# Three slot lists instead of two, experts begun at unit 36, and ScalarE's queue for the rows of early slots

## The chip, the cores and the metric

The kernel runs on one core of one Trainium2 chip. The metric is the device time of one execution, in microseconds (us), lower is better. The engines are TensorE (PE in the profile, its weight loads PEld), VectorE (DVE), ScalarE (ACT), GpSimd (POOL) and SyncE (SP). SP and ACT issue ordinary DMAs, each from a queue of its own; POOL issues the indirect ones (gathers and scatters of rows).

## The reference

Banded attention, then a top-1 mixture of experts on its output. Eight batches, eight heads of 64, 576 positions; heads 0 to 3 see the last 32 positions, heads 4 to 7 every fourth of the last 128. All numbers are float32.

```
scores = np.where(masks, q @ k^T / 8, -1e9)          # per head, masked to the band
x = softmax(scores) @ v  -> [4608, 512]              # 8 batches x 576 tokens
logits = x @ w_gate + modality_bias[modality_id]     # 8 experts
e_idx = argmax(logits); gate_w = softmax(logits)[e_idx]
for e in range(8):
    m = e_idx == e
    out[m] = gate_w[m] * (relu(x[m] @ w1[e]) @ w2[e])   # w1 512x1024, w2 1024x512
```

With the given inputs only experts 1, 6 and 7 receive tokens (1621, 2290 and 697 of them).

## The kernel before

**Attention** is cut into 72 units, nine to a batch, in the order of the list `order`; a unit is 128 query rows of four heads. The loop `for t in range(NU + LAG + 1)` is a software pipeline written out by hand: in its turn t it emits the scores of unit t, the exponentials (L361, tile `pe`) of unit t-1, the transposed probabilities (`pT`, L369) of t-2, the products with v (`po`, L375) of t-3, the store of the rows to DRAM (`x_dram`, from ACT's queue) of t-4 and the gate logits (L419) of t-5. PE, DVE, ACT and SP run what is emitted in exactly that order (`manual_schedule`); POOL mostly too. Loads of q, k and v (tiles `st` and `vw`) for the next batches are issued by SP at fixed turns of a batch, `vw` in many small pieces (L138) with a shift inside SBUF behind them (L144).

**Routing.** Five turns after a batch's last unit, `background(b)` starts; the loop advances it by a step or two in each turn. `gating` finds the expert and rank of each token and scatters token numbers and weights into a DRAM table with a region per expert (POOL, L505). `slot_info` turns the counts of tokens into a list of slots: a slot is 256 tokens of one expert. There are two lists here. The early one is made behind batch 2 (`EARLY_B`), holds six full slots (`NEARLY`) and uses the tokens of batches 0 to 2; the other comes behind batch 7 and holds twelve slots and one half slot. A runtime loop after them takes what may be left.

**A slot** needs: its row of the list read into registers (`TENSOR_LOAD`), the token numbers (`idt`, from the table), four gathers of 128 half rows by POOL (`xr`), a write of these to DRAM (`x_slot`), four loads back in a layout for 32 x 32 transposes (`xg`), two transposes on DVE (`xt`), and a split into two fp32r parts (`xh`, `xl`). In the kernel before, `idt`, `x_slot` and `xg` are all issued by SP. `x_slot`, `xg` and `xr` have one buffer each. The expert's weights come in six pieces (`fetch_weights`: w2 pair 0, w1 half 0, pairs 1 and 2, half 1, pair 3) into single buffers `w1q` and `w2q`; a slot with the same expert as the slot before skips the copies.

**The experts' work** is the generator `slots`: a slot is eight chunks of 128 hidden columns, each twelve matmuls to `pt` (L806), the relu to `hh` (ACT, L812) and `hl` (DVE), and two chunks later six matmuls to `py` (L787). A chunk is four steps. From turn `T_MOE` = 49 on, `step()` weaves these into the attention, 4.4 steps a turn (`MOE_RATE`), so 1.1 chunks a unit. At the start three banks of PSUM for the attention (`ps_o`) become one, and two go to `py`. `ahead(n, f, end)` is called twice in each chunk and issues what the next slots need.

Of the kernel before, what the change touches and what calls it, by code (L numbers as in the profile page):

```python
# [23 lines left out]
NT = B * S  # L24
# [14 lines left out]
NEARLY = 6  # L39
EARLY_B = 2  # L40
NSTAT = 12
HALFF = 4
T_MOE = 49
# [21 lines left out]
def kernel(  # L65
# [379 lines left out]
    def gating(b, lT):  # L445
# [40 lines left out]
        state['counts'] = [run[:, :, 0]] + [oh[:, :, c] for c in range(NGB)]  # L486
# [13 lines left out]
        for c in range(NGB):  # L500
            if c > 0 and b < B - 1:
                yield
                if b != EARLY_B:
                    yield
# [4 lines left out]
            for before in scatters:  # L509
                tc.declare_no_dep(ins, before, reason="every token has a row of its own")  # L510
            scatters.append(ins)
# [3 lines left out]
    def slot_info(counts, early):  # L515

        ps = psum['o'].tile([P, 512], F32, name="po")
# [3 lines left out]
        ns = gwk.tile([1, 1, NE], F32, name="ns")  # L523
        if early:
            nc.vector.tensor_copy(out=cn, in_=ps[0:1, 0:NE])
            nc.vector.tensor_single_scalar(cn, cn, 8, op=ALU.arith_shift_right)
            nc.vector.tensor_copy(out=ns[:, 0, :], in_=cn)
            yield
        else:
# [6 lines left out]
            full = gwk.tile([1, NE], F32, name="full")  # L536
# [16 lines left out]
            nc.vector.tensor_tensor(out=ns[:, 0, :], in0=full, in1=done[:, 0:NE], op=ALU.subtract)  # L553
            yield
        n = NEARLY if early else NSLOT
        cs = gwk.tile([1, 1, NE], F32, name="cs")
        nc.vector.tensor_tensor_scan(out=cs[:, 0, :], data0=one8, data1=ns[:, 0, :], initial=0.0, op0=ALU.mult, op1=ALU.add)
        if early:

            d = done[:, 0:NE]  # L560
            nc.vector.tensor_tensor(out=d, in0=ns[:, 0, :], in1=cs[:, 0, :], op=ALU.subtract)
            nc.vector.tensor_scalar(out=d, in0=d, scalar1=float(NEARLY), scalar2=0.0, op0=ALU.add, op1=ALU.max)
            nc.vector.tensor_tensor(out=d, in0=d, in1=ns[:, 0, :], op=ALU.min)
        yield
# [5 lines left out]
        if not early:  # L570

            nc.vector.tensor_tensor(out=ns[:, 0, :], in0=full, in1=done[:, 1:NE + 1], op=ALU.subtract)
# [5 lines left out]
        if not early:  # L578
            nc.vector.tensor_scalar(out=bs, in0=bs, scalar1=done[:, 0:1], scalar2=None, op0=ALU.add)
        yield  # L580
        state['info_e' if early else 'info'] = slot_list(es, bs, n, "info_e" if early else "info")
# [3 lines left out]
    def rest_info():  # L585
# [5 lines left out]
        nc.vector.memset(state['info'][:, 2, NSTAT:NSTAT + 1], 1)  # L591
# [18 lines left out]
    pool.memset(done, 0.0)  # L610
    last_e = cpool.tile([1, 1], F32, name="last_e")
# [13 lines left out]
    def fetch_ids(si, after=(), nu=2):  # L625

        row = nc.sync.value_load(si[0:1, 1:2], min_val=0, max_val=(NE + 1) * NT - SLOT)
        idt = gat.tile([P, 2, 3], I32, name="idt", bufs=NEARLY)
        load = nc.sync.dma_start(out=idt[:, 0:nu], in_=table[ds(row, P * nu), :].rearrange("(p u) t -> p u t", u=nu))
        wait_all(load.ins, after)  # L630
        return idt, nu

    def gather(n, ids):
# [4 lines left out]
        nrows = (EARLY_B + 1) * S if n < NEARLY else NT + 1  # L638
# [6 lines left out]
        nc.sync.dma_start(out=x_slot[0:P * nu, :].rearrange("(u p) c -> p u c", p=P), in_=xr[:, 0:nu])  # L645
# [4 lines left out]
        for r in range(KC):  # L650
            nc.sync.dma_start(out=xg[BLK * r:BLK * (r + 1), 0:nu * KC],
                              in_=x_slot[0:P * nu, P * r:P * (r + 1)].rearrange("(g i) c -> i g c", i=BLK))
# [30 lines left out]
    early = {}  # L683
    NS = NEARLY + NSTAT + 1
    taken = set()

    def background(b):

        if b < B - 1:
            yield  # L690
        yield from gating(b, state['lT', b])
        if b == EARLY_B:
            yield
            yield from slot_info(state['counts'], True)
            for i in range(NEARLY):
                early['si', i] = slot_regs(state['info_e'], i)
            yield
            yield
            for i in range(3):
                early['ids', i] = fetch_ids(early['si', i])  # L700
                yield
            yield
            early['loads'] = fetch_weights(early['si', 0], True)
            yield from together(islice(early['loads'], 2), gather(0, early['ids', 0]))
            yield
            yield from prepare_x(0, early['ids', 0])
        elif b == B - 1:
            yield
            yield from slot_info(state['counts'], False)
            yield from rest_info()  # L710
            state['routed'] = True
# [57 lines left out]
    def slots(ns, ids_of, ahead, base=0):  # L769
# [25 lines left out]
        for n in range(ns):  # L795
            ids = ids_of[n]
            cols = P * ids[1]
            for f in range(FC):
                g = n * FC + f
                if f == 0:  # L800
                    xh, xl = state.pop(('x', base + n))
# [17 lines left out]
                if g + 2 < ns * FC:  # L819
                    split_w1(g + 2)  # L820
# [5 lines left out]
    ids_of, si_of, fetching = {}, {}, []  # L826

    def fetch_slot(n):

        if n < NEARLY:  # L830
            si_of[n] = early['si', n]
            ids_of[n] = early['ids', n] if n < 3 else fetch_ids(si_of[n])
        elif n < NS:
            half = n == NS - 1
            si_of[n] = slot_regs(state['info_h'], 0) if half else slot_regs(state['info'], n - NEARLY)
# [175 lines left out]
```

## Time and profile before

| | us |
|---|---|
| runs shown | 783.83, 777.83, 779.45 (median 779.45) |
| the profiled execution, its own time | 780.03 |
| its span in the trace | 778.3 |
| PE busy / PEld / DVE / ACT / POOL | 675.1 / 584.1 / 504.8 / 407.2 / 258.9 |
| mean granted TensorE clock | 0.919 |

The 1.7 us between the span and the time lie around the program. The profile names groups by line, engine, operation and tiles as `out<-in`; a wait is given as "engine line waited for", with the total, how often, and the longest. A window row gives the busy time of each engine in a stretch, then the granted clock, the share of the DMA engines' time, and GB/s. Units can be found in it by the exponential of each (`pe<-sm`, ACT), chunks by their relu (`hh`, ACT).

### The profile page before, as it was taken

What the parts mean: (1) busy time and instruction counts of PE and PEld (TensorE: products, weight loads), DVE (VectorE), ACT (ScalarE), POOL (GpSimd) and SP (SyncE); (2) the same over time, 40 slices, a digit from 0 to 9 for tenths busy, and PEclk for the clock granted to TensorE, in tenths of its full rate; (3) what the DMA queues carried; (4) which work ended last, traced back from release to release, by engine and by line L of the source; (5) the groups of instructions that cost most, each with busy time, mean ns of one, the idle gap of its engine ahead of it and who ended that gap; (6) DMA issues with size and microseconds to landing.
All of it is one profiled execution on the core that took longest, in us unless ns stands there. A gap on an engine that the chain in (4) does not pass through costs nothing. (4 is left out here: it accounts for less than half of the span.)

```text
span 778.3 us, 17878 instructions
## 1 busy us (share of the span) xinstructions
PE 675.1 (87%) x6286; PEld 584.1 (75%) x6286; DVE 504.8 (65%) x1216; ACT 407.2 (52%) x900; POOL 258.9 (33%) x348
## 2 busy tenths in 40 slices
PE   5898888883447999988989898999999999999995
PEld 3686767663336877776778787999999999999984
DVE  2587766682245677766857764777666677766763
ACT  3374655551324556653555364566566656656553
POOL 7323534433331433434444523233133323312100
PEclk7598988997659799999999999999999999999998
DMA  9776675759567557982322599332582333266270
GB/s 170 170 183 144 144 164 127 168 133 203 132 165 171 177 122 183 216 201 60 78 76 42 130 277 260 120 109 89 164 227 78 109 97 109 95 177 189 82 186 21
DMA packets 151009, 111.79 MB, mean 144 GB/s; under 512 B 87600, under 2 KB 124978, under 8 KB 150916
## 3 DMA queue, kind: packets, MB, share of 16 engines
q1 hardware_dynamic: 132884, 81.97, 44.6%
q0 software_dynamic: 8048, 19.20, 8.4%
q10 hardware_dynamic: 9984, 9.44, 3.7%
q8 instruction: 50, 0.82, 0.5%
q14 instruction: 43, 0.35, 0.2%
HBM read 127.52 MB, written 29.39 MB: 202 GB/s over the span
## 5 line engine op out<-in xcount | busy, mean ns | idle before, releaser
L806 PE MATMUL pt<-xh,w1h 128*128 128x256 f32 (+1 forms) x608 | 176.9, 291 | 3.5 <-ACT xh L745 3.2
L806 PE MATMUL pt<-xh,w1l 128*128 128x256 f32 (+1 forms) x608 | 172.4, 284 | 5.2 <-DVE w1l L756 4.5
L806 PE MATMUL pt<-xl,w1h 128*128 128x256 f32 (+1 forms) x608 | 172.3, 283 | 1.5 <-DVE xl L746 1.5
L812 ACT ACTIVATE hh<-pt 128x256 fp32r<-128x256 f32 (+1 forms) x152 | 57.6, 379 | 151.5 <-PE pt L806 151.1
L756 DVE TENSOR_TENSOR w2l<-w2q,w2h 128x512 fp32r<-128x512 f32 x152 | 106.1, 698 | 45.0 <-ACT w2h L755 38.0
L806 PEld LDWEIGHTS pt<-xh,w1h 128*128 128x128 f32 x608 | 115.9, 191 | 12.6 <-ACT xh L745 4.1
L284 POOL DMA_INDIRECT xr<-x_dram,idt x74 | 81.4, 1100 | 128.8 <-DMA x_slot<-xr 70.4
L787 PE MATMUL py<-w2h,hh 128*128 128x512 f32 x296 | 124.0, 419 | 0.0
L806 PEld LDWEIGHTS pt<-xl,w1h 128*128 128x128 f32 x608 | 116.2, 191 | 6.8 <-DVE xl L746 1.9
L806 PEld LDWEIGHTS pt<-xh,w1l 128*128 128x128 f32 x608 | 116.6, 192 | 6.1 <-DVE w1l L756 5.9
L787 PE MATMUL py<-w2h,hl 128*128 128x512 f32 x296 | 119.4, 403 | 0.0
L787 PE MATMUL py<-w2l,hh 128*128 128x512 f32 x296 | 117.2, 396 | 0.0
L756 DVE TENSOR_TENSOR w1l<-w1q,w1h 128x512 fp32r<-128x512 f32 x152 | 106.2, 699 | 14.2 <-ACT w1h L755 14.2
L284 POOL TENSOR_TENSOR sm<-sm,nmx 128x384 f32<-128x384 f32 x72 | 61.1, 849 | 137.6 <-DVE den L382 71.0
L813 DVE SCALAR_TENSOR_TENSOR hl<-pt,hh 128x256 fp32r<-128x256 f32 (+1 forms) x152 | 62.7, 413 | 65.8 <-ACT hh L812 65.7
L755 ACT CAST w1h<-w1q 128x512 fp32r<-128x512 f32 x152 | 94.2, 621 | 15.6 <-DMA w1q<-in_moe_w_dram 15.6
L284 POOL DMA_INDIRECT out_dram<-ys,idt x37 | 40.6, 1099 | 179.4 <-ACT ys L790 100.8
L369 ACT COPY pT<-pt 96x512 f32<-96x512 f32 x72 | 41.8, 581 | 102.5 <-PE pt L366 102.4
L755 ACT CAST w2h<-w2q 128x512 fp32r<-128x512 f32 x152 | 93.3, 614 | 0.3
L787 PEld LDWEIGHTS py<-w2l,hh 128*128 128x128 f32 x296 | 56.6, 191 | 13.7
L375 PE MATMUL po<-vw,pT 96*64 96x65 f32 x1152 | 56.1, 244 | 11.3 <-DMA vw<-vw 8.2
L375 PEld LDWEIGHTS po<-vw,pT 96*64 96x64 f32 x1152 | 45.1, 151 | 24.2 <-issue 12.1
(163 smaller groups left out, 1084.9 us busy)
## 6 DMA issues: line engine op xcount, KB each, us to landing
w2q<-in_moe_w_dram SPq DMA_DIRECT2D x76, 512.0 KB
w1q<-in_moe_w_dram SPq DMA_DIRECT2D x152, 256.0 KB
x_slot<-xr SPq DMA_DIRECT2D x18, 512.0 KB
xg<-x_slot SPq DMA_DIRECT2D x72, 128.0 KB
x_dram<-x_sb ACTq DMA_DIRECT2D x32, 256.0 KB
st<-in_k_dram SPq DMA_DIRECT2D x32, 144.0 KB
st<-in_q_dram SPq DMA_DIRECT2D x32, 144.0 KB
st<-in_k_dram SPq DMA_DIRECT2D x16, 288.0 KB
```

Of the source, the lines that this page charges most:

```text
L284: ins = tc.keep_in_program_order(getattr(nc.gpsimd, name)(*args, **kw))
L369: nc.scalar.copy(out=self.pT, in_=src)
L375: nc.tensor.matmul(out=pov[u * TQ:(u + 1) * TQ, h, :], lhsT=self.pT[:, h, u * TQ:(u + 1) * TQ], rhs=self.vts[kd][:, h, i, :], start=True, ...
L755: nc.scalar.copy(out=hi, in_=raw)
L756: nc.vector.tensor_tensor(out=lo, in0=raw, in1=hi.bitcast(F32), op=ALU.subtract)
L787: nc.tensor.matmul(out=py[u], lhsT=ht[:, us], rhs=wt, start=(f + n == 0), stop=(f + n == FC + 1))
L806: nc.tensor.matmul(out=ph, lhsT=wt[:, c, :], rhs=xt[:, c, 0:cols], start=(c + i == 0), stop=(c + i == KC + 1))
L812: nc.scalar.activation(out=hh, in_=ph, func=AF.Relu)
L813: nc.vector.scalar_tensor_tensor(out=hl, in0=ph, scalar=0.0, in1=hh.bitcast(F32), op0=ALU.max, op1=ALU.subtract)
```

## The change

- **Lists.** `EARLY = ((1, 3), (3, 5))`: a list of three slots behind batch 1 (tokens of batches 0 and 1), a list of five behind batch 3 (batches 0 to 3), and one of ten and a half slot behind batch 7. `slot_info(counts, r)` keeps in `done` how many full slots of each expert earlier lists took. The slots remain 19.
- **Start.** `T_MOE` is gone. The experts begin in the turn after `background(1)` has emitted the split of slot 0's rows (`state['go']`), which is turn 36; the kernel before began in turn 49.
- **Queues.** The token numbers of slots 0 and 1, and `x_slot` and `xg` of the eight early slots, are issued from ACT's queue instead of SP's. One more `yield` stands between the last gather of a slot and its `x_slot`.
- **Control.** `ahead` looks at what is there instead of at fixed slot numbers, and `hold` emits no expert step before its rows and weights have been emitted.

```
+EARLY = ((1, 3), (3, 5))
+NEARLY = sum(n for _, n in EARLY)
+NSTAT = 18 - NEARLY
-T_MOE = 49
...
-    def fetch_ids(si, after=(), nu=2):
+    def fetch_ids(si, after=(), nu=2, queue=nc.sync):
-        row = nc.sync.value_load(si[0:1, 1:2], min_val=0, max_val=(NE + 1) * NT - SLOT)
-        load = nc.sync.dma_start(out=idt[:, 0:nu], in_=table[...])
+        row = queue.value_load(si[0:1, 1:2], min_val=0, max_val=(NE + 1) * NT - SLOT)
+        load = queue.dma_start(out=idt[:, 0:nu], in_=table[...])
...
     def gather(n, ids):
-        nrows = (EARLY_B + 1) * S if n < NEARLY else NT + 1
+        nrows = round_rows(n)
+        queue = nc.scalar if n < NEARLY else nc.sync
...
-        nc.sync.dma_start(out=x_slot[0:P * nu, :]..., in_=xr[:, 0:nu])
+        yield
+        queue.dma_start(out=x_slot[0:P * nu, :]..., in_=xr[:, 0:nu])
         yield
...
-            nc.sync.dma_start(out=xg[BLK * r:BLK * (r + 1), 0:nu * KC], ...)
+            queue.dma_start(out=xg[BLK * r:BLK * (r + 1), 0:nu * KC], ...)
...
     def background(b):
+            yield from together(steps, slot_info(state['counts', b], round_of[b]))
+            if round_of[b] > 0:
+                return
+            yield
+            for n in range(2):
+                fetch_slot(n, nc.scalar)
+                yield
+            load_more(0, 1)
+            yield
+            rows = gather(0, ids_of[0])
+            for i, _ in enumerate(rows):
+                yield
+                if i in (1, 3):
+                    load_more(0, 1)
+            yield
+            yield from prepare_x(0, ids_of[0])
+            state['go'] = True
...
     for t in range(NU + LAG + 1):
-        if t == T_MOE:
-            run(tasks_early)
+        if 'go' in state and not moe:
...
-        if t < T_MOE or t >= NU:
-            advance()
+        advance([*round_of, B - 1] if moe and t < NU else range(-1, B))
```

**Slot 0's rows.** On SP before, this stands between the first weights of slot 0 and its rows (`st` and `vw` are loads of later batches; the loads of `xg` follow directly behind):

```order
L123 DMA st<-in_k_dram 48x12x64 x4
L123 DMA st<-in_q_dram 48x12x64 x4
L138 DMA vw_106<-in_v_dram 64x4x64 x2
L138 DMA vw_106<-in_v_dram 16x4x64
L138 DMA vw_106<-in_v_dram 48x4x64
L138 DMA vw_106<-in_v_dram 64x4x64
L138 DMA vw_106<-in_v_dram 32x4x64 x2
L138 DMA vw_106<-in_v_dram 64x4x64
L138 DMA vw_106<-in_v_dram 48x4x64
L138 DMA vw_106<-in_v_dram 16x4x64
L138 DMA vw_106<-in_v_dram 64x4x64 x2
L645 DMA x_slot<-xr 128x2x512
```

In the changed kernel the same two steps stand on ACT, about half a unit apart; the exponentials (L361) are those of units 32 and 33:

```order
L361 ACTIVATE pe<-sm 128x384
L653 DMA x_slot<-xr 128x2x512
L472 ACTIVATE ex<-ex 96x48
L369 COPY pT<-pt 96x512
L401 CAST uxh<-pt 128x256
L320 COPY kT_101<-pt 128x2x144
L318 ACTIVATE qT_100<-po 128x2x144
L659 DMA xg<-x_slot 32x8x128 x4
L361 ACTIVATE pe<-sm 128x384
```

The loads of later batches no longer stand ahead of the rows; the attention's own work now stands behind them on ACT.

**Slot 1's rows**, on ACT of the changed kernel, in the turn 38 (for slots 2 and 3 one instruction stands between the two DMAs; for slots 4 to 7 four to eight do):

```order
L361 ACTIVATE pe<-sm 128x384
L805 CAST w2h<-w2q_240 128x512
L805 CAST w1h<-w1q_238 128x512
L653 DMA x_slot<-xr 128x2x512
L659 DMA xg<-x_slot 32x8x128 x4
L863 ACTIVATE hh<-pt 128x256
L369 COPY pT<-pt 96x512
L401 CAST uxh<-pt 128x256
```

The loads of `xg`, which read what `x_slot` wrote, directly follow it, ahead of a relu and of a unit's transposed probabilities.

**The first expert matmuls**, on PE of the changed kernel against before, right behind the logits (L419) of the unit 31:

```order
 L419 MATMUL po<-uxl,wgs 16x64
-L366 MATMUL pt<-ident,pe 96x128 x4
-L397 MATMUL pt<-ident,x_sb 128x128 x2
-L312 MATMUL pt<-ident,st 128x96 x3
-L312 MATMUL po<-ident,st 128x96 x3
+L857 MATMUL pt<-xh,w1h 128x256
+L857 MATMUL pt<-xl,w1h 128x256
+L857 MATMUL pt<-xh,w1l 128x256
+L857 MATMUL pt<-xh,w1h 128x256
+L857 MATMUL pt<-xl,w1h 128x256
+L857 MATMUL pt<-xh,w1l 128x256
```

From here on the experts' matmuls (L857, L806 before) stand between the attention's; before, only attention follows here for thirteen more turns.

More of the change, by code (lines that the diff above doesn't have):

```diff
@@ L510, in gating @@
                 tc.declare_no_dep(ins, before, reason="every token has a row of its own")
+            for load in state['loads_of_ids']:
+                tc.declare_no_dep(ins, load, reason="the rows of full slots are written before")
             scatters.append(ins)
@@ L838, in ahead @@
[L838 to L852 removed]
+    todo = {'calls': 0, 'ids': 2, 'rows': 1}
```

190 lines of the change are left out of this document (100 added, 90 removed).

## The prediction

> **What bounds the kernel now.** I read the windows first, cut where the work changes; the cuts are starts of a unit's exponential (units 9, 36, 42, 48, 53, 71).
>
> ```profile
> 52.20:154.20 102.00, 84.69 (x1331) 72.56 (x1325) 71.89 (x229) 54.82 (x140) 42.86 (x67) 0.88 0.68 151
> 154.20:172.60 18.40, 16.17 (x287) 13.75 (x284) 16.95 (x67) 11.07 (x31) 7.32 (x10) 1.00 0.58 139
> 172.60:232.30 59.70, 24.12 (x309) 20.25 (x307) 18.20 (x54) 14.28 (x34) 19.18 (x25) 0.66 0.70 162
> 232.30:272.30 40.00, 35.35 (x358) 29.61 (x360) 25.44 (x65) 21.53 (x50) 12.06 (x14) 0.87 0.69 175
> 272.30:391.70 119.40, 109.45 (x1211) 90.41 (x1207) 87.32 (x220) 65.72 (x150) 44.63 (x60) 0.99 0.61 141
> 391.70:480.00 88.30, 76.65 (x508) 66.56 (x507) 58.55 (x157) 42.60 (x90) 37.79 (x41) 0.95 0.57 154
> 502.50:750.50 248.00, 248.00 (x1585) 224.11 (x1584) 174.80 (x306) 149.37 (x308) 62.09 (x56) 1.00 0.45 130
> ```
>
> Columns are length, then busy time of PE, PEld, DVE, ACT, POOL, then clock, DMA share and GB/s. PE fills the last window wholly and nine tenths of the woven ones (232.3 to 391.7). The hole is the third: 59.7 us with 24.1 us of PE work at clock 0.66, just ahead of the first expert matmul. Counts of exponentials (`pe`) and relus (`hh`) in the same windows give the rates:
>
> ```profile
> L361 ACT ACTIVATE pe<-sm x27: 514/526/532, 52.2 to 150.9; 128x384 f32<-128x384 f32 x27
> L361 ACT ACTIVATE pe<-sm x6: 514/521/532, 172.6 to 229.4; 128x384 f32<-128x384 f32 x6
> L361 ACT ACTIVATE pe<-sm x5: 514/520/526, 232.3 to 268.1; 128x384 f32<-128x384 f32 x5
> L361 ACT ACTIVATE pe<-sm x18: 514/522/535, 272.3 to 384.5; 128x384 f32<-128x384 f32 x18
> L812 ACT ACTIVATE hh<-pt x26: 363/384/392, 236.5 to 388.6; 128x256 fp32r<-128x256 f32 x26
> L812 ACT ACTIVATE hh<-pt x88: 377/385/388, 502.5 to 747.8; 128x256 fp32r<-128x256 f32 x88
> ```
>
> Attention alone takes 102.0/27 = 3.78 us a unit, the six units in the hole 9.95 each, a woven unit first 40.0/5 = 8.0 and then 119.4/18 = 6.63, and a chunk of experts alone 248/88 = 2.82. A woven unit carries 1.1 chunks, 3.1 us: weaving hides nearly nothing, since 6.63 - 3.1 = 3.5 is what attention alone costs. So thirteen more woven turns gain nothing by themselves; what can be won is the hole. The timeline says what is in it:
>
> ```profile
> 190.99 0.23 DVE L437 TENSOR_REDUCE dstf<-t 96x6 f32<-96x48 f32 x1 [9.42 <-POOL t L284]
> 192.03 0.92 PE L350 MATMUL pss<-kT,qT 64*64 64x96 f32 x16 [7.89 <-DVE sm L353]
> 187.56 1.07 POOL L284 DMA_INDIRECT xr<-x_dram,idt  x1 [15.55 <-DMA idt<-table]
> 192.56 1.01 POOL L284 DMA_INDIRECT xr<-x_dram,idt  x1 [0.16 <-DVE nmx L356]
> 224.17 0.71 DVE L739 STREAM_TRANSPOSE xt<-xg 128x512 f32<-128x512 f32 x1 [21.45 <-DMA xg<-x_slot]
> 225.25 0.29 PE L419 MATMUL po<-uxl,wgs 128*16 128x128 f32 x1 [21.16 <-DVE uxl L402]
> ```
>
> Two chains. POOL stood 15.55 us before slot 0's first gather for the token numbers; what routing asked of POOL waited behind it, DVE behind POOL, PE behind DVE: 7.89 us. Then DVE stood 21.45 us before slot 0's transpose for `xg`, and PE 21.16 us. Together 29.1 us of PE. Why the rows were late is on SP's timeline:
>
> ```profile
> 178.53 6.35 SPq L629 DMA_DIRECT2D idt<-table  x3
> 201.44 3.83 SPq L123 DMA_DIRECT2D st<-in_k_dram  x4
> 205.36 3.38 SPq L123 DMA_DIRECT2D st<-in_q_dram  x4
> 208.84 7.38 SPq L138 DMA_DIRECT2D vw<-in_v_dram  x12
> 216.39 0.46 SPq L645 DMA_DIRECT2D x_slot<-xr  x1
> 219.30 1.79 SPq L651 DMA_DIRECT2D xg<-x_slot  x4
> ```
>
> ```profile
> DMA to landing us min/median/max: 2.8/4.1/7.1
> ```
>
> The last gather was issued at 193.6 and a gather lands 4.1 us later (the row of `idt`'s readers), at 197.7; `x_slot` left SP at 216.39, 18.7 us later, behind loads of later batches.
>
> **Part by part.** The sum runs over the profiled execution: span 778.3 us, own time 780.03, 0.6 above the median of 779.45.
>
> *Up to unit 36* little changes but one more list: seven tiny matmuls and some twenty DVE operations on one partition, nearest row 0.23 us (`dstf`), so 4.6 us over five units on a DVE busy 71.89 of 102. Cost nothing, with 4.6 if that slack is not there. Unit 36 stands at **154.2**.
>
> *Slot 0's rows now go over ACT.* SP's 18.7 us and the wait for the numbers behind SP's loads go; what is late next are the transfers themselves, and now ACT waits for them, with a unit's `pT` and `uxh` behind it and PE behind these.
>
> ```profile
> DMA to landing us min/median/max: 2.9/6.1/6.9
> 231.84 0.37 ACTq L410 DMA_DIRECT2D x_dram<-x_sb  x1
> ```
>
> The first of these rows is the table's scatters, 6.1 us to land. ACT meets its first `idt` about a unit after the last scatter: 6.1 - 3.8 = 2.3 us. `x_slot` to `xg` was 219.30 - 216.39 = 2.9 us; half a unit (1.9) lies between: 1.0. Four issues of `xg` hold ACT as SP, 1.8 us (a store's issue on ACT, 0.37 us, says the same). The transpose came 224.17 - 219.30 = 4.9 us after the first issue of `xg`; with 1.9 to 3.8 us between in the new order, DVE still waits 2.0. Sum **7.1 us**; bounds 0 (these stretches are DMA-bound and have slack) and 29.1 (both old waits come back). I take 7.1, since its rows are transfers of the same size.
>
> Here one rule speaks against the change. The Trainium skill, page "DMA: Bandwidth & Descriptors", section "Issuing engines are not separate DMA queues", says that DMAs started by SyncE, ScalarE and GpSimd run on the same 16 DMA engines and interleave, and that starting them from several engines only saves the sequencer's time, which is usually small. The trace shows that time as 18.7 us here, not small; by the rule's "usually" it would have stayed and this term were 21.2 instead of 7.1, rival two.
>
> *Woven units.* From unit 36 to 71 there are 35 instead of 23. I price them as before: 40.0 for the first five, then 30 x 6.63 = 199.0: **239.0**. The loss of PSUM banks for attention is in that rate. Bounds: 35 x 6.63 = 232 and 35 x 8.0 = 280.
>
> *Rows of slots 1 to 7 over ACT.* In the order of before SP waits there and nobody cares. ACT now issues 0.4 + 1.8 = 2.2 us a slot, and for slots 1 to 3 the loads of `xg` stand at most one instruction behind `x_slot`, so ACT waits the 2.9 us too: 5.1 a slot. Behind it are a relu, a `pT` and the weight splits. PE has little in hand (three `pt` banks, shared with attention), so I count all of it, 3 x 5.1 = **15.3 us**, and nothing for slots 4 to 7, where a chunk stands between. Bounds 0 (ACT is busy 65.72 of 119.4) and 7 x 5.1 = 36; I stay at the middle, as no row shows an ACT wait of this kind. SP gains these issues, worth nothing while PE bounds.
>
> *Two more weight loads.* Slots now run 1,6,6 / 1,1,6,6,7 / 1... instead of 1,1,6,6,6,7 / 1..., so nine loads instead of seven; those of slots 1, 3 and 5 fall in the woven stretch, where one fell before.
>
> ```profile
> w2q<-in_moe_w_dram SPq DMA_DIRECT2D x76, 512.0 KB
> w1q<-in_moe_w_dram SPq DMA_DIRECT2D x152, 256.0 KB
> 440.00:460.00 20.00, 18.59 (x120) 16.41 (x119) 12.02 (x22) 10.23 (x21) 6.96 (x7) 1.00 0.95 251
> ```
>
> A load is 4 x 512 + 8 x 256 KB = 4.2 MB, 16.7 us at the 251 GB/s of a window that is nearly all weights. Two are 33 us of DMA; the woven windows leave three to four tenths of 239 us free. That hides them but for the crowd at turns 36 to 42, where slot 0's second half and slot 1's whole load meet a batch's `st` and `vw`: **3 us**, bounds 0 and 33.
>
> *The rest.* At unit 71 ACT's order has 41 relus behind it against 26, so 15 chunks fewer remain: 386.6 us of before (778.3 - 391.7) less 15 x 2.82 = 42.3: **344.3**. The end of routing keeps its place: two slots of early rows ahead of it, as before; its 88.3 us window is carried over.
>
> Sum: 154.2 + 7.1 + 239.0 + 15.3 + 3 + 344.3 = 762.9, with 1.7 around it **764.6 us**, 1.9% under the median.
>
> **Rivals.**
>
> 1. *ACT's waits are hidden.* For it: ACT idles 45% of the woven time, and its stores, which also wait, delay nobody today. Against: PE follows ACT closely there. Terms 7.1, 15.3 and 3 become 5, 0 and 0: 742.5, time 744.
> 2. *The wait only changes its place.* The transfers of slot 0's rows share the DMA engines with the loads (share 0.70 in the hole), land as late as before, and ACT or DVE stands for them: 21.2 for 7.1, span 777.0, time 779. This is the rule's case. Against it: SP's 18.7 us were spent before the transfer had been issued.
> 3. *Slower: ACT waits for SP's loads.*
>
> ```profile
> SPq L123 <- DMA x_dram<-x_sb: 32.2, 11, 11.6
> SPq L669 <- DVE w2l L756: 190.0, 58, 12.0
> ```
>
> By these rows loads on SP (L123) waited 32.2 us for stores that ACT had issued, though they share no data: DMAs of the two queues do wait for each other. SP also stands 190 us in all for DVE to free `w2q`. If ACT's `x_slot` or `xg` has to wait for a weight load or `vw` piece that SP has not yet issued, ACT, and with it PE, stands for SP. Without the 15.3 the sum is 747.6; it decides from 40 us on, 5.0 us for each of eight gathers (slower by over 1% then). At 8 us each: 747.6 + 64 + 1.7 = 813. Against it: the stores that ACT issues now show no such wait.
>
> That the change does not do what it says is unlikely: counts of the inputs fill both short lists exactly (3 and 5 full slots), and the order has experts from turn 36.
>
> **How the numbers follow.** A measurement of this kernel tells a change from none at about 1%, 7.8 us: under 771.7 is faster, above 787.2 slower. Forecast 0.48, nearly all of it under 771.7; rival one 0.20; rival two 0.19, inside 1%; rival three 0.11; the rest 0.02. Faster 0.65, same 0.22, slower 0.13. All low ends give 732, all high ends above 840; the range holds the forecast, rival one from 743 on and rival two, up to 786, and leaves out rival three and the corners.
>
> **What would show it.** Right: no PE wait above 8 us before the first expert matmul, which starts near 160; unit 71 near 419; PE waits on ACT of 2 to 5 us at slots 1 to 3 behind an ACT DMA; the last 340 us as before. Wrong: a DVE wait for `xg` of over 10 us (rival two), an ACT DMA held while SP's weight loads run (rival three), woven units well off 6.6, or the end of routing finding no slot ready.

## The result: 3.6% slower, and where the time went

The changed kernel takes **807.28 us** (median of four runs, 803.85 to 813.67); the kernel before took 779.57 beside it. The ratio is **1.0355, 95% interval 1.0293 to 1.0416**. The forecast was 764.6, so the sign was wrong. Ratios and intervals leave out single executions that lie more than 1.5% above the fastest of their kernel, among them one of e4 that took 1237.58 us, whose trace is not used. The profiled execution of the changed kernel is the longest of its four (813.67, span 811.9, 0.8% above the median). Its windows are cut at starts of unit exponentials (9, 28, 36, 38, 53, 71); the last one is a stretch of experts alone:

```profile
56.20:127.70 71.50, 59.22 (x957) 50.67 (x951) 52.57 (x183) 38.40 (x98) 29.75 (x46) 0.90 0.73 142
127.70:182.30 54.60, 34.51 (x421) 28.84 (x417) 28.02 (x81) 20.54 (x50) 20.75 (x29) 0.72 0.91 191
182.30:216.60 34.30, 12.11 (x122) 10.03 (x122) 7.69 (x20) 6.83 (x17) 5.90 (x6) 0.69 0.77 180
216.60:334.70 118.10, 103.78 (x1072) 86.90 (x1065) 77.92 (x207) 60.01 (x138) 37.52 (x47) 0.89 0.64 145
334.70:470.30 135.60, 118.92 (x1208) 98.74 (x1208) 86.56 (x224) 65.60 (x151) 46.88 (x60) 0.90 0.64 144
557.80:783.70 225.90, 225.68 (x1441) 204.33 (x1440) 158.77 (x278) 135.64 (x279) 59.68 (x54) 1.00 0.53 144
```

The same view of before, for units 28 to 36:

```profile
122.10:154.20 32.10, 25.30 (x397) 21.45 (x392) 21.71 (x70) 16.28 (x43) 14.57 (x23) 0.89 0.72 159
```

The third row after is the old hole in a new place: 34.3 us with 12.1 us of PE work at clock 0.69. The second row shows that it begins earlier: eight units take 54.6 us instead of 32.1, with nearly the same number of matmuls (421 against 397) and the clock at 0.72 instead of 0.89. Against the forecast's sum, term by term:

| stretch | forecast | measured | difference |
|---|---|---|---|
| to unit 28 | 122.1 | 127.7 | +5.6 |
| units 28 to 36 | 32.1 + 7.1 | 54.6 | +15.4 |
| units 36 to 38, first experts | 2 x 8.0 | 34.3 | +18.3 |
| units 38 to 71 | 33 of the 35 woven units (223.0), 15.3 and 3 | 253.7 | +12.4 |
| unit 71 to the end | 344.3 | 341.6 | -2.7 |
| span | 762.9 | 811.9 | +49.0 |

What stands in the first of these holes, on the timeline of the changed kernel (SP's DMA issues, then ACT, then PE):

```profile
172.88 2.46 SPq L123 DMA_DIRECT2D st<-in_k_dram  x4
175.45 5.41 SPq L123 DMA_DIRECT2D st<-in_q_dram  x4
180.96 11.60 SPq L138 DMA_DIRECT2D vw<-in_v_dram  x12
...
193.40 1.87 SPq L674 DMA_DIRECT2D w1q<-in_moe_w_dram  x4
...
203.23 0.62 ACT L805 CAST w1h<-w1q 128x512 fp32r<-128x512 f32 x1 [15.55 <-DMA w1q<-in_moe_w_dram]
203.41 0.37 ACTq L653 DMA_DIRECT2D x_slot<-xr  x1
210.88 1.88 ACTq L659 DMA_DIRECT2D xg<-x_slot  x4
212.81 0.38 ACT L863 ACTIVATE hh<-pt 128x256 fp32r<-128x256 f32 x1 [8.96 <-issue]
...
213.72 0.74 PE L312 MATMUL pt<-ident,st 96*128 96x96 f32 x3 [22.19 <-ACT pT L369]
```

ACT stood 15.55 us for the second half of slot 0's `w1`, which SP issued at 193.40, behind a batch's `st` and `vw` (172.88 to 192.56). Then ACT issued slot 1's `x_slot`, and all that follows in its order stood until `xg` could go at 210.88, 7.5 us later; by the built program this first `xg` waits for `x_slot` to land and for nothing else. PE stood for both: 22.19 us. It is the same pattern as before, a list's data behind a batch's loads, with ACT's own DMA added. The DMA engines had room until SP issued the weights, and were full from then on:

```profile
187.00:193.40 6.40, 4.53 (x44) 3.56 (x42) 1.60 (x3) 0.68 (x2) 1.14 (x1) 1.00 0.27 60
193.40:203.20 9.80, 0.00 (x0) 0.00 (x0) 0.00 (x0) 0.00 (x0) 0.00 (x0) 0.61 1.01 235
```

Through the woven units ACT stands again and again (waits of ACT from unit 38 to 71, total, times, longest; the relu is named since it is next in ACT's order):

```profile
ACT hh L863 <- DMA xg<-x_slot: 14.5, 2, 8.3
ACT hh L863 <- DMA w2q<-in_moe_w_dram: 6.6, 1, 6.6
ACT hh L863 <- DMA vw<-in_v_dram: 4.6, 1, 4.6
```

The longest of them on the timeline:

```profile
314.67 6.93 ACTq L659 DMA_DIRECT2D xg<-x_slot  x4
321.65 0.38 ACT L863 ACTIVATE hh<-pt 128x256 fp32r<-128x256 f32 x1 [8.33 <-DMA xg<-x_slot]
```

Four issues that take 1.9 us where nothing holds them took 6.9. The built program says what the later ones wait for. This is ACT's order around that place, slot 3's rows:

```
387 L653 DMA x_slot<-xr 128x2x512 [waits DMASW7_49,DMAHW5_49,DMASW6_49,DMAHW7_49,DMASW1_49,DMASW0_49]
388 L318 ACTIVATE qT_100<-pt 128x2x144 [waits PE_49]
389 L659 DMA xg<-x_slot 32x8x128 [waits DMAHW7_49,DMAHW3_49]
390 L659 DMA xg<-x_slot 32x8x128
391 L659 DMA xg<-x_slot 32x8x128 [waits DMAHW2_49]
392 L659 DMA xg<-x_slot 32x8x128 [waits DMAHW3_49]
```

A semaphore is a counter that an instruction can wait for. In this program SP's and ACT's DMAs signal their completion on eight shared ones (DMAHW0 to 7), and a DMA that is to signal on one waits until the DMA that used it last has landed, also when the other engine has yet to issue that one. Here the first `xg` waits for `x_slot` (DMAHW7) and an `st` of SP (DMAHW3), the third for a `w1q` piece, the fourth for the first `xg` itself. All but the wait for `x_slot` have nothing to do with the data.

### The profile page after: what moved, and what is told of

Its sections match the earlier page's. It is cut to its first block, busy times and chain, and to the rows that moved or that the text cites. A ratio compares the mean times of both kernels' runs of the same rounds, so it can differ in the third digit from the quotient of the medians.

```text
span 811.9 us, 17892 instructions
## 1 busy us (share of the span) xinstructions
PE 690.8 (85%) x6293; PEld 595.8 (73%) x6293; DVE 508.6 (63%) x1243; ACT 406.5 (50%) x900; POOL 260.3 (32%) x348
## 5 line engine op out<-in xcount | busy, mean ns | idle before, releaser
L857 PE MATMUL pt<-xh,w1h 128*128 128x256 f32 (+1 forms) x608 | 183.6, 302 | 16.8 <-DVE hl L864 5.9
L857 PE MATMUL pt<-xh,w1l 128*128 128x256 f32 (+1 forms) x608 | 176.6, 290 | 5.7 <-DVE left L597 5.1
L857 PE MATMUL pt<-xl,w1h 128*128 128x256 f32 (+1 forms) x608 | 176.2, 290 | 1.8 <-DVE xl L796 1.8
L857 PEld LDWEIGHTS pt<-xh,w1h 128*128 128x128 f32 x608 | 120.2, 198 | 26.5 <-DVE hl L864 6.1
L806 DVE TENSOR_TENSOR w2l<-w2q,w2h 128x512 fp32r<-128x512 f32 x152 | 104.5, 687 | 42.7 <-ACT w2h L805 36.5
L837 PE MATMUL py<-w2h,hh 128*128 128x512 f32 x296 | 126.5, 427 | 0.0
L857 PEld LDWEIGHTS pt<-xl,w1h 128*128 128x128 f32 x608 | 120.7, 198 | 6.5 <-DVE xl L796 2.3
L857 PEld LDWEIGHTS pt<-xh,w1l 128*128 128x128 f32 x608 | 120.5, 198 | 6.5 <-DVE left L597 5.3
L806 DVE TENSOR_TENSOR w1l<-w1q,w1h 128x512 fp32r<-128x512 f32 x152 | 106.7, 702 | 21.8 <-ACT w1h L805 21.8
L312 PE MATMUL pt<-ident,st 96*128 96x96 f32 x273 | 44.7, 281 | 37.1 <-ACT pT L369 27.7
L312 PEld LDWEIGHTS pt<-ident,st 96*128 96x128 f32 x273 | 34.4, 162 | 44.5 <-ACT pT L369 28.8
```

What stands on the lines that cost most here:

```text
L312: nc.tensor.transpose(out=pt[:, 2 * PQ * i:2 * PQ * (i + 1)], in_=src[:, s].rearrange("p a d -> p (a d)"), identity=ident[:2 * PQ, :2 * PQ])
L806: nc.vector.tensor_tensor(out=lo, in0=raw, in1=hi.bitcast(F32), op=ALU.subtract)
L837: nc.tensor.matmul(out=py[u], lhsT=ht[:, us], rhs=wt, start=(f + n == 0), stop=(f + n == FC + 1))
L857: nc.tensor.matmul(out=ph, lhsT=wt[:, c, :], rhs=xt[:, c, 0:cols], start=(c + i == 0), stop=(c + i == KC + 1))
```

## The experiments

All ratios are against the kernel before, run beside it on the same chip. The quoted expectations name the kernels in full (h2_after_slot0 is h2, built from the changed kernel; h1_before_slot0 is h1, built from the kernel before). Two theories come up again and again: "queue" says that the loss is ACT standing at its own DMAs, "crowd" that loads which meet in one place delay each other whatever queue they come from.

### All rows on SP, and the kernel before with rows on ACT

**Edit e1** (on the changed kernel):

```
-        queue = nc.scalar if n < NEARLY else nc.sync
+        queue = nc.sync
-                fetch_slot(n, nc.scalar)
+                fetch_slot(n, nc.sync)
```

> The changed kernel, with every DMA of the early slots issued by SP again; lists, start at turn 36 and weight loads stay. Theory 'queue' (ACT stands for x_slot and for SP's loads; the gaps ahead of ACT's idt and xg issues sum to some 36 us, and xg's issues to 14): most of that goes, 765 to 775 us, no ACT wait ahead of a DMA, and the PE wait of 22 us at 191 shrinks by the 7.5 us between x_slot and xg. Theory 'crowd' (turn 36 follows directly on a batch's st and vw loads, so the weights of slots 0 and 1 and these loads stand in each other's way whatever queue the rows take): 795 to 815, with slot 0's rows now late behind SP, as before the change, and the wait for w1q still there.

Measured 788.05, ratio 1.0071 (1.004 to 1.0102), between the ranges of both theories. The queue accounts for most of the loss. What remains around the start is the old chain, DVE's wait for `xg` (120 to 230 us) with PE 16.2 us behind it:

```profile
DVE xt L789 <- DMA xg<-x_slot: 23.3, 2, 17.6
```

**Edit e2** (on the kernel before: `x_slot` and `xg` of its six early slots and the first two `idt` on ACT):

```
+        queue = nc.scalar if n < NEARLY else nc.sync
-        nc.sync.dma_start(out=x_slot[...
+        queue.dma_start(out=x_slot[...
-            nc.sync.dma_start(out=xg[...
+            queue.dma_start(out=xg[...
```

> The kernel before (two lists, start at turn 49), with x_slot and xg of its six early slots and the first two idt issued by ACT. Theory 'queue': the waits on ACT cost more than the hole gives back, 785 to 800. Theory 'crowd': the hole of 29 us shrinks to under 10 and the rest stays, 755 to 770; then the queue was the good part of the change.

Measured 793.39, ratio 1.0107 (1.0047 to 1.0168). The hole did shrink: units 42 to 48 ran from 177.8 to 213.2, 35.4 us instead of 59.7. But units 48 to 71 took 189.7 instead of 159.4. The three largest of ACT's waits on DMAs from 170 us on:

```profile
ACT w2h L756 <- DMA w2q<-in_moe_w_dram: 14.4, 1, 14.4
ACT kT L320 <- DMA xg<-x_slot: 8.8, 2, 6.8
ACT hh L813 <- DMA xg<-x_slot: 6.5, 1, 6.5
```

The queue that shortened slot 0's wait lengthened the rest; the next two kernels take the two apart.

### Only slot 0 on ACT

**Edits h1 and h2** (h1 on e2, h2 on the changed kernel):

```
-        queue = nc.scalar if n < NEARLY else nc.sync
+        queue = nc.scalar if n < 1 else nc.sync
```

> The kernel before with only slot 0's rows (x_slot, xg) and the first two idt on ACT's queue; slots 1 to 5 stay on SP. 'Queue' (an ACT DMA of the rows holds ACT, and PE with it, wherever SP's loads are under way; only slot 0 is worth it): the hole keeps the 24 us it lost when all six slots went over ACT (units 42 to 48 in about 35 us instead of 59.7), units 48 to 71 come back from 189.7 to about 160, time near 757. 'Crowd' (the DMA engines are full, so what arrives early at one place is late at the next): the 20 us gap behind the start, where ACT waited for the first weights behind a batch's vw pieces, stays, units 48 to 71 take 175 to 190, time 772 to 785.

> The changed kernel with only slot 0's rows and the ids on ACT's queue; slots 1 to 7 on SP. 'Queue': units 36 to 38 as in the changed kernel (a gap near 20 us for the weights), then 7.1 us a unit as with everything on SP instead of 7.7: 33 x 0.6 = 19 us less, time near 788. 'Crowd': the woven units stay near 7.7, since it is the two more weight loads that fill them, time near 803. If ACT's hold of slot 0 alone were the loss of units 28 to 36, unit 36 still stands at 182.

h1 measured 772.32, ratio **0.9865** (0.979 to 0.994): faster than both kernels, though short of the 757 that "queue" expected. In its windows (units 42 to 48, then 48 to 71) the hole keeps its 25 us, and the woven part takes 175.1 instead of 159.4:

```profile
181.40:215.80 34.40, 23.32 (x304) 20.04 (x304) 17.89 (x53) 14.24 (x34) 15.12 (x21) 0.66 0.98 201
215.80:390.90 175.10, 147.73 (x1563) 122.11 (x1564) 113.58 (x284) 87.51 (x199) 56.48 (x73) 0.90 0.60 146
```

Of these 15.7 us, 15.2 are one PE gap at 233.7, where ACT waits 11.4 us for the second piece of slot 0's `w2q`, which SP issued behind a batch's loads, and then 6.2 for a `w1q`: "crowd" was right on that point.

h2 measured 783.59, ratio **1.0027** (0.9981 to 1.0073). Taking slots 1 to 7 off ACT's queue gives back 3.3% of 779.6, some 26 us of the 28 lost. Its windows (units 28 to 36, 36 to 38, 38 to 71):

```profile
124.40:178.20 53.80, 35.22 (x418) 29.74 (x416) 27.63 (x80) 20.43 (x49) 20.81 (x28) 0.71 0.98 198
178.20:203.40 25.20, 12.17 (x124) 10.10 (x123) 7.64 (x21) 6.77 (x17) 1.97 (x2) 0.78 0.74 174
203.40:437.80 234.40, 210.21 (x2270) 174.98 (x2262) 165.15 (x429) 125.89 (x287) 89.84 (x110) 0.94 0.70 163
```

The 33 woven units went from 253.7 to 234.4, 7.69 to 7.10 each. Of these 19.3 us only 6.8 are less standing of PE; in the other 12.5 PE was busy for longer on the same work (222.7 against 210.2, at clock 0.89 and 0.90 against 0.94). The profiled execution of h2 lies 0.6% below its median, that of the changed kernel 0.8% above, so the two profiles differ by more than the medians do. The start is no shorter in its first part: eight units still take 53.8.

### Which DMA holds ACT

**Edits h8, h9 and h10**, all on the changed kernel: h8 moves `x_slot` of slots 1 to 7 to SP and leaves `xg` on ACT, h10 the other way round, h9 puts two more turns between them.

```
h8   -        queue.dma_start(out=x_slot[...
     +        (queue if n < 1 else nc.sync).dma_start(out=x_slot[...
h9   +        for _ in range(2 if 0 < n < NEARLY else 0):
     +            yield
              while 0 < n < NS and n - 1 not in taken:
h10  -            queue.dma_start(out=xg[...
     +            (queue if n < 1 else nc.sync).dma_start(out=xg[...
```

> The changed kernel with x_slot of slots 1 to 7 on SP; xg of these slots, four DMAs each, stays on ACT. Slots 1 to 7 on ACT cost 24 us (after against h2_after_slot0). 'It is the wait for x_slot to land, in front of xg, and the four issues': nothing or little is gained, 800 to 807. 'It is the x_slot DMA that ACT holds for (its gathers have not landed)': most of the 24 us is gained, 783 to 789.

> The changed kernel with the xg DMAs of slots 1 to 7 issued two turns later, 8 to 16 ACT instructions behind x_slot instead of 1 to 9, still on ACT. 'Landing' (ACT waits for x_slot, 2.9 us alone and 5 to 8 us with loads running, as it stands too near): the wait in front of the first xg goes, 790 to 798. 'Shared semaphores' (each xg waits for a load that SP issued before it, wherever it stands): ACT's gaps stay as large, 800 to 810. 'Issue time' (each xg takes ACT 0.5 to 1 us, with no wait): 803 to 808.

> The changed kernel with x_slot of slots 1 to 7 on ACT and xg of these slots on SP (slot 0 wholly on ACT). 'xg holds ACT' (four issues and the wait for x_slot's landing in front of them): the ratio falls to that of h2_after_slot0, 1.00 to 1.01. 'Either holds it, as both wait for transfers that are not done': 1.02 to 1.03. 'It is not the hold': 1.03 to 1.04.

h8: 828.88, ratio 1.0492 (1.0442 to 1.0543), worse than the changed kernel and above both expectations: ACT's `xg` now also waits for an `x_slot` that stands in SP's queue. At 378 us ACT's timeline shows one such `xg`, and the relu behind it had waited 19.27 us. h9: 814.47, ratio 1.0289 (1.024 to 1.0339), against 1.0355 not surely different. h10: 781.31, ratio **0.9988** (0.9946 to 1.003), as good as h2. So in the changed kernel `x_slot` on ACT costs nothing measurable, and **it is `xg` on ACT that costs**.

How it costs is only partly shown. In the changed kernel's trace ACT stands some 13 us ahead of the `xg` of slots 1 to 4 until `x_slot` has landed, 6 until the first piece of the same `xg` has, and 6 for SP's `vw` and `w2q` pieces (slots 5 and 6). In h9 most of this is gone: ACT's waits for DMAs in units 42 to 71 are these two, where the three rows of the changed kernel shown in the section on the result sum to 25.7:

```profile
ACT hh L865 <- DMA w1q<-in_moe_w_dram: 2.7, 2, 2.2
ACT kT L320 <- DMA st<-in_k_dram: 1.8, 1, 1.8
```

Even with the 10.7 us of h9 for which the profile names no releaser this is a fall of some 10 us, yet these units take 218.1 us against 222.6 in the changed kernel, 202.7 in h10 and 201.2 in h2. So ACT's standing at its DMAs is not the whole price of `xg` on ACT; what the rest is stays open.

**Edit h15** asks the same of the kernel before (slot 0 and the ids on ACT, `x_slot` of slots 1 to 5 on ACT, their `xg` on SP), and h14 is h1 again beside it.

> The kernel of h1_before_slot0 (before, with slot 0's rows and the first two idt on ACT's queue) in more rounds on another chip; it is the version that beat both kernels. 'Queue for slot 0 alone': ratio 0.98 to 0.99 again. 'Noise of one chip': 0.995 to 1.005.

> The kernel before with slot 0 and the first two idt on ACT, and x_slot of slots 1 to 5 on ACT as well, their xg on SP. 'Only xg holds ACT' (as h10_after_xs_act says of the changed kernel): as h14_before_slot0_again, 0.98 to 0.99. 'x_slot holds it here too': between that and e2_before_act's 1.011, 0.995 to 1.011.

h14: 780.15 on a chip where the kernel before takes 790.49, ratio **0.9869** (0.9838 to 0.99), so slot 0 alone over ACT is a gain of 1.3%. h15: 0.9933 (0.9907 to 0.996). It falls between the two expectations. Of the 2.4% between e2 and h14, 1.7 go with `xg`; the 0.6 that `x_slot` costs here is small, but not nothing.

### The same rows over POOL

**Edits h3 and h4** (`nc.gpsimd` in place of `nc.scalar` for the rows, h3 in the changed kernel, h4 in e2). POOL's DMAs signal on semaphores of their own.

> The changed kernel with the rows of slots 0 to 7 (x_slot, xg) issued by POOL instead of ACT. POOL's transfers signal completion on semaphores of their own, which SP's and ACT's do not use; so a row transfer can no longer wait for a load of SP, and an SP load not for it. 'Queue by shared semaphores': ACT is held no more, woven units 7.1 us or less, unit 36 earlier than 182, time 775 to 788. 'Queue by transfer time' (the hold is the landing of x_slot alone): POOL is held as ACT was, its next gathers and the routing work behind it are late, woven units 7.3 to 7.7, time 790 to 807. 'Loads': 11 us above the kernel before whatever the queue, 790.

> The kernel before with the rows of its six early slots issued by POOL (the first two idt on ACT). 'Queue by shared semaphores': the hole shrinks as with ACT's queue (units 42 to 48 in about 35 us) and units 48 to 71 keep the 159 us of before: time 750 to 758. 'Queue by transfer time': the hole shrinks, units 48 to 71 take 170 to 190 as POOL stands for the transfers and the gathers behind it are late: 770 to 793. 'Crowd': the 20 us gap for the first weights stays: 770 to 780.

h3: 799.78, ratio 1.0212 (1.0132 to 1.0293). h4: 792.1, ratio 1.0132 (1.006 to 1.0205), as with ACT's queue. In h3 POOL stands for the transfers (waits of POOL and of PE between 120 and 480 us), and PE stands behind DVE for what routing asks of POOL (DVE waits 20.8 us for POOL there):

```profile
POOL x_slot L653 <- DMA xr<-x_dram,idt: 25.5, 4, 10.7
PE po L480 <- DVE oh L471: 22.0, 1, 22.0
```

Separate semaphores are thus no cure, though the loss is smaller than with ACT's queue (1.0355): POOL, too, stands for the landing when it issues a transfer before its source has landed.

### The two more weight loads

**Edits e3 and h13** (e3 on the changed kernel, h13 on h2). They leave the weight copies of slots 1 and 3 out by clearing their flag, so that slots 1 to 4 run on slot 0's weights; the instructions are the same but for one `memset` in each list.

```
         state['info', r] = slot_list(es, bs, n, f"info{r}")
+        if early:
+            at = 1 if r == 0 else 0
+            nc.vector.memset(state['info', r][:, 2, at:at + 1], 0)
```

> The changed kernel, but the copies of the weights of slots 1 and 3 are left out (these slots compute with the weights that lie there), so seven loads as before the change. Theory 'queue': 800 to 806, as the loads were hidden. Theory 'loads' (two more loads of 4.2 MB fill the DMA engines in the woven stretch): 775 to 785. Theory 'crowd': slot 1's load is a part of the crowd, 790 to 800, with the wait for w1q at 203 us unchanged, since that one is slot 0's.

> The kernel of h2_after_slot0 without the weight copies of slots 1 and 3 (their flag for a new expert is cleared; the matmuls run on slot 0's weights). With ACT's queue the same edit gave 1.0355 to 1.0137. 'Loads cost on their own': the ratio falls by 0.010 to 0.015 to about 0.99. 'Loads cost only through ACT's holds' (they delay the row transfers that ACT stands for): it stays at 1.00.

e3: 796.09, ratio 1.0137 (1.0079 to 1.0194), 2.2% under the changed kernel, in the range that "crowd" gave. h13: 772.06, ratio 0.9854 (0.9766 to 0.9942), 1.7% under h2, a little more than expected. The loads cost on their own, some 13 us, not only through ACT. The 33 woven units of h13:

```profile
206.30:427.00 220.70, 204.58 (x2276) 169.45 (x2272) 165.06 (x430) 125.82 (x287) 89.51 (x110) 0.98 0.61 138
```

That is 6.69 us a unit, where h2 had 7.10: DMA's share goes from 0.70 to 0.61 and the clock from 0.94 to 0.98. Of the 13.7 us, 5.6 are PE busy for less time, 8.1 less standing.

### Why the start is slow even then

**Edits e4, h6 and h7**: all six pieces of slot 0's weights go out at the start instead of some of them behind the next batch (e4 on the changed kernel, h7 on h2, h6 on h1).

```
e4, h7  -            load_more(0, 1)
        +            load_more(0, 2)
h6      -            yield from together(islice(early['loads'], 2), gather(0, early['ids', 0]))
        +            run(islice(early['loads'], 3))
        +            yield
        +            yield from together(islice(early['loads'], 3), gather(0, early['ids', 0]))
```

> The changed kernel, with all six pieces of slot 0's weights emitted in turns 30 to 32 instead of three there and three in turns 36 and 37, so ahead of the next batch's st and vw loads on SP. Theory 'crowd': the 15.6 us wait of ACT for w1q at 203 us goes, 785 to 797, unless the loads of st behind it become late by as much. Theory 'queue': at most the overlap of that wait with ACT's own, 800 to 808.

> The kernel before with slot 0's rows on ACT's queue (as in h1_before_slot0) and all six pieces of slot 0's weights issued by SP at the start instead of two, so that the last four no longer stand behind the next batch's st and vw loads. 'Behind the batch' (the 15 us gap at the start is the weights' wait in SP's order): the gap goes to under 5 us, time 757 to 762. 'Crowd' (the DMA engines are full there): the st and vw of the next batch land later by what the weights took, attention stands for them instead; time within 5 us of h1_before_slot0, 768 to 777.

> The changed kernel with slots 1 to 7 on SP (as h2_after_slot0) and all six pieces of slot 0's weights issued by turn 32. 'Behind the batch': the 13 us gap where ACT waits for w1q is gone, time 768 to 773. 'Crowd': the gap only changes its place, 780 to 787.

e4: 803.42, ratio 1.0271 (1.0217 to 1.0326), where "queue" had it. h6: 784.51, ratio 0.9917 (0.9884 to 0.995), no better than h1. h7: 804.72 where the kernel before takes 790.6, by the medians 1.018; its runs spread from 795 to 809, so there is no interval, but the best of them is at 1.006, no better than h2's 1.0027, and the median is above both expectations. The wait for `w1q` is gone and another has come, in DVE's waits of h7 around the start:

```profile
DVE xt L789 <- DMA xg<-x_slot: 27.0, 1, 27.0
```

That is the `xg` of slot 1, now the one that stands behind the batch's loads on SP.

**Edit h12** (on h2) loads slot 0's weights earlier, from a constant expert (its issues fall in units 24 to 29 instead of 33 to 37, so not the 15 units earlier that were meant), and **edit h11** (on h2) holds the experts back until unit 41:

```
h12  +        if b == 0:
     +            loads_of[0] = [None, 6]
     +            yield from fetch_weights(None, True)
h11  -        if 'go' in state and not moe:
     +        if 'go' in state and not moe and t >= 41:
```

> The changed kernel with slots 1 to 7 on SP (as h2_after_slot0) and experts held back until unit 41, while slot 0's rows and weights are fetched where they were. 'Start in the hole' (PE stands because experts begin before their weights are there, and attention alone could have filled the time): the 13 us gap goes, ratio 0.985 to 0.995. 'Crowd' (attention itself waits there for st and vw, which share the DMA engines with slot 0's weights and rows): units 28 to 41 take as long, ratio 1.00 to 1.01.

> The kernel of h2_after_slot0 with slot 0's weights loaded some 15 units earlier, from a constant expert (the routing is not known by then, so this load is no part of a usable kernel), between two batches' loads. It takes 4.2 MB out of the stretch of units 28 to 38. 'Crowd of bytes': units 28 to 38 take 79 us in h2_after_slot0 against 38 in the kernel before and come down by 15 to 20; time ratio 0.98 to 0.99. 'It is the rows and the ids alone': ratio 1.00, and the wait is then for xg.

h12: 792.14, ratio 1.0156 (1.0068 to 1.0245). Both theories missed: units 28 to 38 take 75.4 us instead of 79.0 and not 15 to 20 less, and the time went up. SP's timeline shows another piece late: the twelve issues of `vw`, which took 7.4 us in the hole of before, now span 22, and slot 1's `xg` stands behind them:

```profile
187.72 21.99 SPq L138 DMA_DIRECT2D vw<-in_v_dram  x12
...
219.87 1.80 SPq L659 DMA_DIRECT2D xg<-x_slot  x4
```

DVE's waits in the same stretch:

```profile
DVE xt L792 <- DMA xg<-x_slot: 28.5, 2, 23.3
```

The 22 us are not the issues themselves, which take 0.3 to 0.6 us each here as before, but for one of 1.36. They are one wait in front of the tenth, and in these 13.5 us the DMA engines were nearly idle (share 0.14):

```profile
SPq L138 <- DMA x_dram<-x_sb: 13.5, 1, 13.5
194.50:208.00 13.50, 13.32 (x156) 10.98 (x154) 7.65 (x15) 8.12 (x18) 2.28 (x2) 1.00 0.14 44
```

By the built program this `vw` piece is to signal on the semaphore (DMAHW5) that a store of ACT, `x_dram`, used last, and ACT issued that store only at 205.89. The data have nothing to do with each other. In h7, too, SP's `st` and `vw` at this place wait 6.0 and 6.3 us for such stores, and in the changed kernel 4.0 of the 11.60 us of its `vw` row above are one.

h11: 781.58, ratio 1.0015 (0.9976 to 1.0054), no different from h2. With no expert in them, its units 28 to 36 and 36 to 42 take 43.1 and 30.7 us, against 32.1 and 18.4 in the kernel before, and the hole follows in units 42 to 48 (63.5 us), where its experts begin:

```profile
124.90:168.00 43.10, 28.45 (x378) 23.95 (x379) 23.65 (x74) 17.55 (x44) 19.63 (x27) 0.78 0.86 196
168.00:198.70 30.70, 27.08 (x336) 23.47 (x334) 20.79 (x59) 15.50 (x39) 9.74 (x13) 0.81 0.80 143
```

In h7, h11 and h12 the hole thus changes its place and does not go: whichever piece is put ahead, another is late. Two causes are seen, and the runs do not say how much is due to each: SP's order, held up by ACT's stores as in h12, and full DMA engines. For the second the bytes speak. In units 28 to 36 the changed kernel and the one before moved, by the part on DMA packets for these two stretches:

```profile
DMA packets 19296, 10.45 MB, mean 191 GB/s; under 512 B 14186, under 2 KB 17497, under 8 KB 19289
```

```profile
DMA packets 11601, 5.10 MB, mean 159 GB/s; under 512 B 9036, under 2 KB 11340, under 8 KB 11596
```

At 191 GB/s the 5.35 MB more take 28 us; the stretch became 22.5 longer. This is an estimate, as some of these bytes are loads of the next batch, which a longer stretch also lets in.

## Why the prediction was wrong, by its steps

- **Slot 0's rows over ACT, 7.1 us: this step failed, and it is the largest.** The reasoning that SP's 18.7 us were the cause was half right: e2 and h1 show that ACT's queue takes 24 to 25 us out of the hole of before. But the step took the transfers at their durations in the hole and placed them in units 28 to 36, which had DMA at 0.72 and were taken to have slack. With them DMA's share rose to 0.91 (in h2 0.98), and each of the step's waits came out longer:

```profile
ACT pT L369 <- DMA table<-pay,dst: 4.6, 1, 4.6
147.34 0.44 ACTq L653 DMA_DIRECT2D x_slot<-xr  x1
154.72 1.87 ACTq L659 DMA_DIRECT2D xg<-x_slot  x4
DVE xt L789 <- DMA xg<-x_slot: 8.3, 1, 8.3
```

  ACT waited 4.6 us ahead of the first `idt` instead of 2.3; `x_slot` and `xg` are 7.4 us apart, of which ACT stood 3.9 instead of 1.0; DVE waited 8.3 instead of 2.0. With the 1.9 of the issues that is 18.7 instead of 7.1. In units 36 to 38 (+18.3) it is the load of slot 0's second half behind the next batch. The prediction had named this crowd, in the term of the weight loads, and priced it at 3 us. In h2, where only slot 0 goes over ACT, units 28 to 38 still take 79.0 us where the forecast had 55.2.
- **Rows of slots 1 to 7 over ACT, 15.3 us: the wait ahead of `xg` was named, but the size came near by luck in the woven part and was too small in all.** Woven units went from 253.7 to 234.4 without it: 19.3, of which only 6.8 are PE standing, as the step had priced it, and 12.5 PE at work for longer at a lower clock. By the ratios of the changed kernel and h2 the whole edit is 26 us, since it also lengthens the start (units 28 to 38: 88.9 against 79.0). The step counted the landing of `x_slot` at slots 1 to 3 alone, and nothing at slots 4 to 7. PE stood 9.2 us in all behind the `xg` of slots 4 to 6 (slots 6, 4 and 5 in this order), two of which waited for SP's loads:

```profile
PE pt L857 <- ACT pT L369: 3.5, 1, 3.5
PE pt L312 <- ACT pT L369: 3.2, 1, 3.2
PE pt L857 <- ACT qT L318: 2.5, 1, 2.5
```

- **Two more weight loads, 3 us: mis-sized, 13.** The step counted free DMA share (three to four tenths of the woven windows) as cover for 33 us of transfers. h13 shows that it covers only a part: 234.4 against 220.7. The bound of 33 us held.
- **Woven units at 6.63: right, once these two are out.** h13 has 6.69. With 24 for the first three units and 199 for thirty, the forecast had 223.0 for these 33; h13 has 220.7. The 12.4 of the table is thus 4.0 from ACT (19.3 for 15.3), 10.7 from the loads (13.7 for 3) and -2.3 from the rate.
- **The rest, 344.3: right** (341.6).
- **Up to unit 36, "costs nothing": not settled.** Unit 28 is 5.6 us later in this profile and 2.3 in h2's, and the 0.8% by which this execution is above its median is of that size.
- **What would show it.** No PE wait above 8 us before the first expert matmul: right to the letter (the longest is 4.2), but that matmul stood at 175.09, not 160, and the 22 us came right after it. PE waits of 2 to 5 us at slots 1 to 3: 5.9 at slot 3, a part of the 22 at slot 1, under 3 at slot 2; those at slots 4 to 6 were not foreseen. Unit 71 near 419: it was at 470.3. An ACT DMA held while SP's loads run was the sign given for rival three, and it is there.
- **The rivals.** Rival three, "ACT waits for SP's loads", had the right engine and sign and a time of 813, at a chance of 0.11. But its price was too high for its own mechanism, 64 us against the 26 measured: with the forecast's other terms that gives 764.6 - 15.3 + 26 = 775, still no loss. The loss needed the start and the weight loads as well. What spoke against it, that ACT's stores show no such wait, did not carry over to `xg`; and of ACT's standing ahead of `xg` only some 6 us were for SP's loads. Its sign in the other direction, SP's loads that wait for ACT's stores, is what h12 ran into. Rival two went with a rule of the Trainium skill, page "DMA: Bandwidth & Descriptors", section "Issuing engines are not separate DMA queues", which says that DMAs started from several engines run on the same DMA engines and interleave, and that starting them from several engines saves only the time that it takes to issue them, usually little. For slot 0 what was saved was not little: 1.3% (h1 against before), as the 20 issues of a batch's `st` and `vw` stood ahead of its rows in the kernel before (201.44 to 216.22 us). The first half agrees with units 28 to 36, where the DMA share rose from 0.72 to 0.91 when slot 0's rows and weights came in. Rival two's 779 was 28 us short: it kept the forecast's 15.3 and 3 for the rows of slots 1 to 7 and the weight loads.

**The version that beats both** is the kernel before with slot 0's rows alone on ACT's queue: 0.9865 and 0.9869 on two chips. Held against the changed kernel by these ratios, it is 4.7% faster.

## What to carry to other kernels

A DMA that is moved to another engine's queue carries its waits with it: before moving it, ask what the new engine has behind it, and let a busy engine issue only transfers whose source has long landed and whose neighbours on the same completion semaphores are done (here `x_slot` passed, `xg` did not). The waits run both ways: a load on SP can stand for a store that ACT has yet to issue, with the DMA engines idle. A hole that is made of transfers does not go when the work is begun earlier; it moves to where the same bytes now meet, so price the new place with its own DMA share plus the bytes that come, not with the durations from the old one. Free DMA share as a mean over a woven stretch covered only a part of two loads of 4.2 MB here.

## What the runs showed of the hardware that was not expected

- A DMA of SP can wait for a DMA of ACT that shares no data with it, and the other way round, since both signal on the same eight semaphores: 13.5 us at one `vw` piece in h12, with the DMA engines 0.14 busy. The twelve `vw` issues spanned 7.4 us in the hole of before, 11.6 in the changed kernel and 22.0 in h12, while one issue took 0.3 to 0.6 us in nearly all cases.
- The granted clock was lower in the windows in which PE stood more: 0.89 to 0.72 in units 28 to 36, where the busy time of PE rose from 25.30 to 34.51 us for 6% more matmuls; in the woven part 0.98, 0.94 and about 0.89 in h13, h2 and the changed kernel, where PE stood 16.1, 24.2 and 31.0 us. So a stall was paid for again in slower matmuls; that the stall sets the clock is read from these windows and was not tested by itself.
- h2 and h13, whose matmuls are the same, differed by 13.7 us in a stretch in which the DMA engines were on average 0.70 busy in h2. By GB/s times length h13 moved some 7.7 MB less there.
